# Second layer's values of two and a half token blocks by seven products, with weights' sums made as attention begins

## The chip, the cores and the metric

The kernel runs on one core of one Trainium2 chip. The metric is the device time of one execution in microseconds (us); smaller is better. Before the change the median of three runs is 1869.21 us (1868.77 to 1869.33).

## The reference

Two identical layers, each an attention block followed by a gated linear unit, on 2048 tokens of 448 features in float32; both layers use the same weights. There are 16 heads of 28 features.

```python
qkv = (x @ wqkv).reshape(B, S, 3, H, Dh).transpose(2, 0, 3, 1, 4)
q, k, v = qkv[0], qkv[1], qkv[2]
scores = jnp.einsum("bhqd,bhkd->bhqk", q, k) * (Dh ** -0.5)
o = jnp.einsum("bhqk,bhkd->bhqd", _softmax(scores), v)
attn = o.transpose(0, 2, 1, 3).reshape(B, S, D) @ wo
# glu: (sigmoid(x @ w_gate) * (x @ w_up)) @ w_down
x = x + attn(_layernorm(x)); x = x + glu(_layernorm(x))   # twice
```

## The kernel before

Float32 products are made from float16 pieces: each operand is a high and a low part, and a product is high x high + high x low + low x high. The tokens lie in four blocks of 512 (`Block`, b = 0 to 3), each of four tiles of 128 (j = 0 to 3); the 448 features lie in three chunks of 128 and a tail of 64, whose high and low parts share the 128 rows.

**Stages.** For each layer: `project` makes queries, keys and values of all four blocks; `attend` runs 16 heads; then follow the output projection and the gated unit. Layer 0's attention begins at about 117 us, layer 1's projection runs from about 944 to 1037 us.

**Queries and keys by seven products.** In layer 1 `qk_sums` forms them by a Strassen-like scheme: a 2 x 2 split of features and columns, seven products in place of eight, with sums of weights made beforehand (`split_sums`, `add_up`: 13 operations on DVE and 3 copies on POOL for one set of 28 tiles) and sums of activations made by `Block.half_steps` (r11, t1, t2, t3, r21, t4, r22, r12, last_low, last_rows). The activations' sums lie in the tiles `xwide` (four) and `xshort`. Each product goes to a `chain` bank, which adds up and is copied out by ACT several times on the way, or to a `side` bank, which DVE adds in.

**Squares.** Each finished tile of queries and keys is split (`qkhl`), stored, squared on ACT (`sq`) and reduced by two max operations on DVE; short matmuls on PE (`norms`) then make norms of them, from which comes a bound on the scores. With `defer=True`, `qk_sums` leaves a part of its last operations to be called from outside (`fin(False)`); otherwise it does them itself before it returns. `fin()` reads the norms' peaks.

**Values.** `values_product` makes one tile of 128 tokens: 11 matmuls of 448 columns, `vp<-wv,x`, with the tokens as the stationary operand, so each has a weight load of 128 x 128 tokens. `vals` runs it over tiles and copies the bank out (ACT in general, DVE where a bank is named); it calls what stands in `after` behind a tile. The weights lie in `wv`, the tail's in `wv_tail`, which shares the tile `wsums`. The steps of block three (`h3`) run between those tiles of block one and the query products of block two.

**The end of `project`.** After the four blocks' queries and keys, `vals(2, ...)` makes block two's values; behind its second tile comes `guard_of_norms` (bound, guard row, write to `g_scr`), behind its fourth `worst_of_heads` (a small matmul `bounds`, and DVE's `flag`). Then ACT loads its exponential (`warm`), two tiles of block three follow, and all engines read `flag` and branch (`loose`; the branch isn't taken here). Behind the branch SP loads head 0's guard rows and head 1, and the third tile is made. The fourth is made inside the attention (`last_values`).

**The attention's start.** `attend` issues scores in groups of three tiles on PE (`sc`), exponentials on ACT (`prob`), and the products with the values (`acc`). Some score tiles per head go to DVE instead (`score_aside`: nine operations on `aside`, `expo`, `whole`, `power`); their PSUM bank is shared by the next aside of that head. `last_values` is called around the third group. PE's order is fixed by the order of the code, as is every engine's: each runs its instructions in order.

**Storage.** SBUF tiles come from numbered slots, taken from the front of a list and put back at its end (`Slots`); a tile that takes a slot waits for the last reader of the one before it. In layer 0 `split_v` frees the raw weights.

## Time and profile before

| | before |
|---|---|
| median of 3 runs | 1869.21 us |
| the profiled execution's own time | 1869.45 us |
| its span | 1867.7 us |
| PE busy | 1861.4 us |
| ACT busy | 1404.2 us |
| DVE busy | 1462.4 us |
| granted TensorE clock | 1.00 |

A row of the timeline begins with its start in us from the span's start and its length, then engine, line, operation, output and inputs with their shapes, and xN for N like instructions that follow each other; in brackets is how long the engine was idle before and who released it. A row of the waits' chain has start, length, engine, and the group. A row by source line has shortest, median and longest duration in ns, then first and last start. PE is TensorE's matmul, PEld its weight load, PEq and SPq the sequencers. A window's row gives the engines' busy us and counts, the granted clock, the share of the DMA engines and GB/s. A row of DMA issues ends in the KB of one and the median us from issue to landing.

### The profile page before, as it was taken

The numbers are of one execution on the slowest core, as the hardware profiler recorded it, in microseconds if no ns is written. First come the engines' busy times: TensorE is split into PE (matmuls) and PEld (weight loads), VectorE is DVE, ScalarE is ACT, GpSimd is POOL, SyncE is SP. The second block draws the span as 40 slices with busy tenths as digits, with TensorE's granted clock in tenths as the row PEclk, the third lists the DMA queues.
The fourth block names the chain that finished last, engine by engine and source line by source line (L and its number), as shares of the span: only waits on it lengthen the run. The fifth ranks groups of instructions, "written<-read, shape, count | busy, mean of one in ns | idle before, by whom it ended". The sixth has DMA issues, their size and how long they took to land. (4 is left out here: it accounts for less than half of the span.)

```text
span 1867.7 us, 57157 instructions
## 1 busy us (share of the span) xinstructions
PE 1861.4 (100%) x24479; PEld 1416.1 (76%) x24479; DVE 1462.4 (78%) x2933; ACT 1404.2 (75%) x1865; POOL 306.4 (16%) x582
## 2 busy tenths in 40 slices
PE   9999999999999999999999999999999999999999
PEld 4455566656565899999987568888877668999999
DVE  7748898998997888788877477777777688887764
ACT  6569999999993655555567899999999746555541
POOL 3001123453412111212122000000000031121110
PEclk9999999999999999999999999999999999999999
DMA  7674454454433866757764322122120258677653
GB/s 265 182 214 130 131 160 128 125 156 113 136 129 86 288 211 229 244 204 257 243 187 109 88 52 52 27 53 52 30 50 14 79 165 264 210 249 239 235 201 144
DMA packets 114885, 286.24 MB, mean 153 GB/s; under 512 B 15134, under 2 KB 68878, under 8 KB 114496
## 3 DMA queue, kind: packets, MB, share of 16 engines
q0 software_dynamic: 35088, 174.86, 27.8%
q1 hardware_dynamic: 78384, 106.27, 20.3%
q8 instruction: 194, 3.18, 0.7%
q10 hardware_dynamic: 1152, 1.38, 0.3%
q14 instruction: 67, 0.55, 0.1%
HBM read 218.20 MB, written 54.29 MB: 146 GB/s over the span
## 5 line engine op out<-in xcount | busy, mean ns | idle before, releaser
L1574 ACT ACTIVATE prob_s<-sc 128x1536 f32<-128x1536 f32 (+1 forms) x657 | 888.1, 1484 | 5.9 <-PE sc L1559 3.0
L1609 PE MATMUL acc<-prob_s,val_s 128*32 128x256 f32 (+3 forms) x7708 | 587.2, 384 | 0.0
L1559 PE MATMUL sc<-qp_s 114*32 114x512 f16 x7868 | 571.3, 379 | 0.0
L1559 PEld LDWEIGHTS <-qp_s 114*32 114x32 f16 x8192 | 309.9, 96 | 168.8 <-issue 70.8
L1609 PEld LDWEIGHTS acc<-prob_s,val_s 128*32 128x32 f32 x7708 | 314.1, 110 | 100.3 <-issue 9.2
L1944 PE MATMUL dnp<-dn_s,hparts_s 128*128 128x224 f16 x2184 | 245.8, 259 | 0.0
L664 PEld LDWEIGHTS <-gue_s 128*128 128x128 f16 x2240 | 218.8, 98 | 24.5 <-PE op L1738 0.7
L1944 PEld LDWEIGHTS <-hparts_s 128*128 128x128 f16 x2184 | 210.2, 98 | 5.1
L664 PEld LDWEIGHTS <-gul_s 128*128 128x128 f16 x2016 | 197.0, 98 | 19.9
L664 PE MATMUL chain<-xwide_s,gue_s 128*128 128x256 f16 x1680 | 210.9, 273 | 0.0
L1589 DVE SCALAR_TENSOR_TENSOR power_q<-power_q,expo_q 128x512 f32<-128x512 f32 x243 | 168.2, 692 | 8.3
L664 PE MATMUL side<-xshort_s,gul_s 128*128 128x256 f16 x1344 | 165.0, 273 | 0.0
L2017 ACT COPY one_q<-chain 128x256 f32<-128x256 f32 x224 | 83.1, 372 | 105.4 <-PE chain L664 104.6
L2033 DVE TENSOR_TENSOR one_q<-side,one_q 128x512 f32<-128x512 f32 x112 | 74.3, 689 | 39.1 <-PE side L664 38.8
L1638 DVE STREAM_TRANSPOSE oturned_q<-acc 128x512 f32<-128x512 f32 x32 | 23.0, 717 | 98.4 <-PE acc L1609 98.2
L2044 ACT ACTIVATE one_q<-one_q 128x512 f32<-128x512 f32 x56 | 35.3, 630 | 79.8 <-DVE one_q L2033 79.8
L1609 PE MATMUL acc<-power_q,val_s 128*32 128x256 f32 (+3 forms) x300 | 94.2, 396 | 0.0
L1584 DVE TENSOR_SCALAR expo_q<-aside,base 128x512 f32<-128x512 f32 x81 | 60.6, 748 | 40.5 <-PE aside L1559 40.1
L587 POOL TENSOR_SCALAR rs<-mv 128x1 f32<-128x1 f32 x8 | 1.5, 191 | 505.8 <-DVE mv L585 505.8
L664 PE MATMUL chain<-xshort_s,gul_s 128*128 128x256 f16 x672 | 82.5, 273 | 0.0
L1902 DVE TENSOR_TENSOR hparts_s<-hsums_q,hparts_s 128x256 f16<-128x256 f32 (+1 forms) x152 | 71.3, 519 | 11.1 <-ACT hparts_s L1898 11.1
L664 PE MATMUL side<-xwide_s,gue_s 128*128 128x256 f16 x560 | 79.4, 273 | 0.0
(273 smaller groups left out, 2559.0 us busy)
## 6 DMA issues: line engine op xcount, KB each, us to landing
gue_s<-gu_early POOLq DMA_DIRECT2D x52, 960.0 KB, 5.3
gul_s<-gu_late POOLq DMA_DIRECT2D x52, 768.0 KB, 4.7
dn_s<-dn_parts POOLq DMA_DIRECT2D x42, 784.0 KB, 6.7
qp_s<-qk_scr SPq DMA_DIRECT2D x96, 224.0 KB
xt_scr<-xs_s SPq DMA_DIRECT2D x48, 224.0 KB
xraw_s<-xt_scr SPq DMA_DIRECT2D x12, 768.0 KB
qk_scr<-qkhl_q SPq DMA_DIRECT2D x28, 256.0 KB
qp_s<-qk_scr SPq DMA_DIRECT2D x64, 112.0 KB
```

The costliest lines, as they stand in the source:

```text
L664: nc.tensor.matmul(pm, a, x, start=(first and i == 0), stop=(i == len(terms) - 1), skip_group_check=True)
L1559: nc.tensor.matmul(ps[32 * j:32 * j + 32, :], hd.k[:, keys], hd.q[:, qb * W:(qb + 1) * W], start=True, stop=True, tile_position=(0, 32 * j))
L1574: nc.scalar.activation(prob[:, 0:n, :], ps[:, 0:n, :], AF.Exp, scale=exp_scale)
L1584: nc.vector.tensor_scalar(y, ps, base2[:, 0:1], -116.0, op0=ALU.mult, op1=ALU.max)
L1589: nc.vector.scalar_tensor_tensor(p, p, c[k], y, op0=ALU.add, op1=ALU.mult)
L1609: nc.tensor.matmul(acc[qb * VC:(qb + 1) * VC, s], v[:, kc % TB, h, :], probs[c * NB + qb][:, s], start=(kc == 0 and a == 0), stop=(kc == N ...
L1638: nc.vector.transpose(turned.rearrange("p b c -> p (b c)"), acc)
L1902: nc.vector.tensor_tensor(to[:, :, 1], a, to[:, :, 0], op=ALU.subtract)
L1944: nc.tensor.matmul(pm, a[:, x, t], w[:, p, y], start=(begin and n == 0 and (j == 0 or alone)), stop=(n == 2), skip_group_check=True)
L2017: nc.scalar.copy(to, pm)
L2033: nc.vector.tensor_tensor(one[m], side[m], one[m], op=ALU.add)
L2044: nc.scalar.activation(out, v, AF.Sigmoid, scale=gate_scale)
```

## The change

**Values by sevens.** In layer 1, the values of blocks one and two and of tiles 0 and 2 of block three are made by the seven products of `terms_of_halves`: tiles t and t + 2 together, 128 tokens at a time, 38 matmuls of 224 columns for two tiles in place of 22 of 448. The order of products is 0, 1, 2, 4, 3, 5, 6, with two groups taken in turn in `by_sevens`. ACT copies the chain bank out after products 0, 2, 3 and 5; DVE adds the side bank after 3, 4 and 6.

**Weights' sums.** `split_values(0)` and `(1)` make them from the raw value weights in layer 0's attention, on either side of the last value tile, and POOL writes them to `vs_early` and `vs_late`; `load_products` loads them at the start of layer 1's projection. The raw weights are held until then, with the tail in the first place.

**Orders.** `qk_sums(1)` leaves its squares to run between the value products; `h3` moves later; the guard's zero rows are written earlier; at the end of layer 1's projection the order is tile 1 of block three, block two, the products 0, 1, `worst_of_heads`, product 2 of block three's half, the branch, then products 3 to 6.

```diff
+        def split_values(self, j):
+            t = big.get("vpack", [P, N_SUMS, DV], F16)
+            v = self.raw[2].rearrange("p s (z h n) -> p s z h n", z=2, h=2)[:, :, :, j]
+            split_sums(t, v, up[:, 2:3])
+            for to, a, b in ((vs_early[:, j, 0:7], 1, 8), (vs_early[:, j, 7:EARLY], 14, 22),
+                             (vs_late[:, j, 0:6], 8, 14), (vs_late[:, j, 6:LATE], 22, 28)):
+                nc.gpsimd.dma_start(to, t[:, a:b])
+            big.put(t)
...
+        class Values:
...
+            def product(self, k, pm):
+                c = slice(self.s * P, self.s * P + P)
+                pm = pm.rearrange("p (j n) -> p j n", j=2)
+                terms = terms_of_halves(wq.part, self.blk, k)
+                for i, (a, x) in enumerate(terms):
+                    nc.tensor.matmul(pm, x[:, c], a, start=(k < 2 and i == 0),
+                                     stop=(i == len(terms) - 1), skip_group_check=True)
...
+            def on_chain(self, k, z, t):
+                self.product(k, self.chain)
+                nc.scalar.activation(self.to(z, t), self.of(self.chain), AF.Copy, scale=PS)
+
+            def plus(self, i, z, t):
+                v = self.to(z, t)
+                nc.vector.scalar_tensor_tensor(v, self.of(self.side[i]), PS, v, op0=ALU.mult,
+                                               op1=ALU.add)
...
+        def by_sevens(b, blk, after):
+            groups = [Values(b, blk, s, ((0, 1), (2, 3))[s]) for s in range(2)]
+            for k in (0, 1, 2, 4, 3, 5, 6):
+                for g in groups:
+                    g.do(k)
+                for do in after.get(k, ()):
+                    do()
+            blk.drop()
...
-            fin = qk_sums(1, b1, {0: h2[6:7], 1: h2[7:8], 3: h2[8:9], 4: h2[9:10]})
-            vals(1, b1, {1: both(fin, h3[0]), 2: both(*h3[1:3]), 3: both(*h3[3:5])}, banks=order)
-            fin = qk_sums(2, b2, {0: h3[5:6], 1: h3[6:7], 2: h3[7:8], 3: h3[8:9], 4: h3[9:10]},
+            fin = qk_sums(1, b1, {0: h2[6:7], 1: h2[7:8], 3: h2[8:9], 4: h2[9:10]}, None, True)
+            todo = lambda fin=fin: fin(False)
+            by_sevens(1, b1, {0: [todo], 1: [todo], 2: [todo, h3[0]], 4: h3[1:2], 3: [todo],
+                              5: h3[2:3], 6: [fin]})
+            fin = qk_sums(2, b2, {0: h3[3:5], 1: h3[5:6], 2: h3[6:7], 3: h3[7:8], 4: h3[8:10]},
...
-        vals(2, blks[2], {layer: guard_of_norms, 3: worst_of_heads})
-        nc.scalar.activation(warm, warm, AF.Exp)
-        vals(3, blks[3], {}, range(2))
...
+            vals(3, b3, {}, [1], banks={1: 4})
+            by_sevens(2, b2, {1: [guard_of_norms]})
+            group = Values(3, b3, 0, (6, 7))
+            group.do(0)
+            nc.scalar.activation(warm, warm, AF.Exp)
+            group.do(1)
+            worst_of_heads()
+            group.do(2)
         loose = nc.values_load(flag[0:1, 0:1], min_val=0, max_val=1)
...
-        vals(3, blks[3], {}, [2], 0 if layer == 0 else 7)
+        if layer == 0:
+            vals(3, blks[3], {}, [2], 0)
+        else:
+            for k in (3, 4, 5, 6):
+                group.do(k)
...
         begun = last_values()
+        if layer == 0:
+            wq.split_values(0)
...
             if g == 2:
                 last_values(begun)
+                if layer == 0:
+                    wq.split_values(1)
```

On ACT, behind block one's last query and key products in layer 1, before the change (line, operation, output<-inputs, shape; `val_s` are the copied values):

```order
L957 ACTIVATE sq_q_19484<-qkhl_q_19410 128x512
L957 ACTIVATE sq_q_19488<-qkhl_q_19467 128x512
L941 ACTIVATE qkhl_q_19492<-two_q_19380 128x512
L957 ACTIVATE sq_q_19497<-qkhl_q_19472 128x512
L957 ACTIVATE sq_q_19501<-qkhl_q_19492 128x512
L1136 ACTIVATE val_s_18869<-vp_19505 128x16x28
L477 CAST xwide_s_19546<-xraw_s_19254 128x256 x2
L1136 ACTIVATE val_s_18869<-vp_19518 128x16x28
L479 CAST xwide_s_19546<-t_q_19547 128x512
```

and after it, at the same place:

```order
L1001 ACTIVATE sq_q_19537<-qkhl_q_19463 128x512
L1209 ACTIVATE val_s_18918<-vchain_19541 128x8x28
L1209 ACTIVATE val_s_18918<-vchain_19543 128x8x28
L1001 ACTIVATE sq_q_19557<-qkhl_q_19520 128x512
L985 ACTIVATE qkhl_q_19571<-two_q_19433 128x512
L1209 ACTIVATE val_s_18918<-vchain_19541 128x8x28
L1209 ACTIVATE val_s_18918<-vchain_19543 128x8x28
L1001 ACTIVATE sq_q_19588<-qkhl_q_19525 128x512
L480 CAST xwide_s_19592<-xraw_s_19307 128x256 x2
L482 CAST xwide_s_19592<-t_q_19593 128x512
L1209 ACTIVATE val_s_18918<-vchain_19541 128x8x28
L1209 ACTIVATE val_s_18918<-vchain_19543 128x8x28
```

The copies of the chain banks now stand between the squares, and the third pair of them behind the cast of `t_q`. On DVE at that place, after the change:

```order
L989 SCALAR_TENSOR_TENSOR qkhl_q_19571<-two_q_19433,qkhl_q_19571 128x512
L1005 TENSOR_TENSOR sq_q_19588<-sq_q_19588 128x2x128
L1005 TENSOR_TENSOR sq_q_19588<-sq_q_19588 128x2x64
L472 TENSOR_TENSOR t_q_19593<-xraw_s_19307 128x256 x2
L1213 SCALAR_TENSOR_TENSOR val_s_18918<-vside_19542,val_s_18918 128x8x28
L1213 SCALAR_TENSOR_TENSOR val_s_18918<-vside_19544,val_s_18918 128x8x28
```

There `t_q` stands behind two max operations, and the first additions of the side banks behind it. On PE at the end of layer 1's projection, after the change, between the small matmul `bounds` and the reading of the flag:

```order
L1344 MATMUL bounds_20350<-ident,bnd_20199 1x16
L1198 LDWEIGHTS xwide_s_19592
L1198 MATMUL vchain_20336<-vse_s_18931,xwide_s_19592 128x224
...
L1198 LDWEIGHTS xwide_s_19592
L1198 MATMUL vchain_20336<-vse_s_18931,xwide_s_19592 128x224
L1362 TENSOR_LOAD flag_20200
L1363 COMPARE_AND_BRANCH
```

The lines left out are three more such pairs: five matmuls of 224 stand there now, where 22 of 448 stood. On DVE at the start of layer 0's attention, before the change (`val_s` are the copies of block three's third and fourth tile of values, `aside` the first score tile that DVE takes):

```order
L1138 TENSOR_SCALAR val_s_234<-vp_4856 128x16x28
L1138 TENSOR_SCALAR val_s_234<-vp_4903 128x16x28
L1584 TENSOR_SCALAR expo_q_5002<-aside_4997,base_104 128x512
L1585 TENSOR_SCALAR whole_q_5003<-expo_q_5002 128x512
L1586 TENSOR_TENSOR expo_q_5002<-expo_q_5002,whole_q_5003 128x512
```

and after it (the two tiles `vpack_s` take the same slot one after the other):

```order
L292 TENSOR_TENSOR vpack_s_4913<-vpack_s_4913 64x112
L1182 TENSOR_SCALAR val_s_236<-vp_4906 128x16x28
L269 TENSOR_TENSOR sums_q_4966<-wraw_s_158 128x224
L269 TENSOR_TENSOR sums_q_4966<-sums_q_4966,wraw_s_158 128x224
L269 TENSOR_TENSOR sums_q_4967<-wraw_s_158 128x224
L269 TENSOR_TENSOR sums_q_4967<-wraw_s_158,sums_q_4966 128x224
L275 TENSOR_SCALAR vpack_s_4965<-wraw_s_158,up 128x224
...
L292 TENSOR_TENSOR vpack_s_4965<-vpack_s_4965 64x112
L1689 TENSOR_SCALAR expo_q_5051<-aside_5046,base_106 128x512
```

Before the change `expo_q<-aside,base` followed directly on the copy `val_s<-vp`; now thirteen operations stand between them, and thirteen ahead of that copy.

109 lines of the change are left out of this document (79 added, 30 removed).

## The prediction

> **What bounds the kernel now.** I read the page's busy times first, then the chain that ended last, then windows over the stages that the change touches.
>
> ```profile
> PE 1861.4 (100%) x24479; PEld 1416.1 (76%) x24479; DVE 1462.4 (78%) x2933; ACT 1404.2 (75%) x1865; POOL 306.4 (16%) x582
> PE 44%; DVE 0%; issue 0%
> core 0: us, PE busy (x) PEld busy (x) DVE busy (x) ACT busy (x) POOL busy (x), PEclk, DMA share, GB/s
> 982.50:991.30 8.80, 8.80 (x61) 4.76 (x59) 7.92 (x24) 6.96 (x15) 2.08 (x3) 1.00 0.36 99
> 1021.80:1030.80 9.00, 9.00 (x62) 4.73 (x59) 5.44 (x17) 5.15 (x11) 5.42 (x7) 1.00 0.61 166
> 121.50:149.20 27.70, 27.70 (x524) 16.03 (x520) 16.71 (x31) 27.37 (x22) 2.13 (x4) 1.00 0.80 262
> ```
>
> PE is busy throughout, and the part of the chain that the view resolves is PE's. Time falls by what is taken from PE and rises by any hole made in it. The first window is the second layer's values of block one (counted from zero, as in the code): PE full, but DVE at 7.92 of 8.80 us and ACT at 6.96, so little room for more of their work. The second is the same for block two, with room. The third is the first head of layer 0's attention: ACT 27.37 of 27.70, so PE and ACT are both full; only DVE has 11 us free.
>
> **1. The products.** Gone are 44 matmuls of 448 columns for each of blocks one and two and 22 for half of block three: 110. In their place stand 76, 76 and 38: 190 of 224 columns.
>
> ```profile
> 1036.40 1.14 PE vp L1118 x6
> 1835.21 29.34 PE dnp L1944 x306
> L1944 PEld LDWEIGHTS <-hparts_s 128*128 128x128 f16 x2184 | 210.2, 98 | 5.1
> ```
>
> The first row gives 1.14/6 = 0.190 us for one of 448; the second has the very shape that is added (224 columns, a 128x128 load each): 29.34/306 = 0.0959 us. 110 x 0.190 = 20.9, 190 x 0.0959 = 18.2: **-2.6 us**, -1.0 for each whole block and -0.5 for the half. That is all the change can gain. The third row shows 80 more loads of 98 ns; they cost nothing where they run beside matmuls, as 306 pairs in 29.34 us do (98 + 96 in turn would be 59).
>
> [...]
>
> **2. Block one: squares between products.** The seven products of a token tile share two banks. The chain bank is copied out by ACT after the first, third, fifth and sixth in order, and a product that adds to it waits for the copy; a side bank waits for DVE. I set 0 at 982.46, where these values begin. The two groups alternate, five or six matmuls each: the fifth products end at 4.98, the sixth at 6.13, the seventh at 7.28, without the 14 short norm matmuls (0.44).
>
> ```profile
> 982.46 0.73 PE L1118 MATMUL vp<-wv_s,xwide_s 128*128 128x448 f16 x3
> 982.27 0.60 ACT L941 ACTIVATE qkhl_q<-alone 128x512 f16<-128x512 f32 x1
> 983.28 1.15 ACT L957 ACTIVATE sq_q<-qkhl_q 128x512 bf16<-128x512 f16 x2
> 986.14 0.52 ACT L1136 ACTIVATE val_s<-vp 128x448 f32<-128x448 f32 x1
> 988.48 0.62 ACT L479 CAST xwide_s<-t_q 128x512 f16<-128x512 f32 x1 [0.77 <-DVE t_q L469]
> 984.45 1.01 DVE L961 TENSOR_TENSOR sq_q<-sq_q 128x256 bf16<-128x256 bf16 x4
> 987.71 0.74 DVE L469 TENSOR_TENSOR t_q<-xraw_s 128x256 f32<-128x256 f32 x2
> 992.67 0.63 ACT L981 COPY one_q<-chain 128x256 f32<-128x256 f32 x2
> ```
>
> In the new order a cast of t_q stands on ACT before the two copies after the fifth product. It waits for a DVE pair (0.74), which stands behind two max operations (0.50), which wait for ACT's square of one_q (0.58). Ahead of that square ACT has three activations of 512 (about 0.5 apart), two squares (1.15) and four copies (0.32 to 0.35 each, from the pair of 256 in 0.63): about 4.4 from 982.27, so the square ends near 4.8, the pair at 6.0, the cast at 6.4 or, with the pipelining that the overlapping rows show, 5.9, and the first copy at 6.2 to 6.8. The sixth product would start at about 5.0 and waits 1.2 to 1.8. I take the low end: the rows' starts lie closer than their durations. DVE's addition into the side bank ends near 7.65, so the seventh waits some 0.3 more: **+1.6**. The steps of block three, spread over later tables, take DVE's and ACT's room in the two next products; no row shows them late, and I take 0, with one more DVE pair (0.74) as the worst and the old spacing as the best.
>
> **3. Block two** has the same turns with idle neighbours: copy 0.35, about 0.3 for the last matmul to end and PE to restart, against a cover of about 0.5: **+0.1**, and 0.2 for the norms that now come before tile one's products: **+0.3**. The guard's zero memset and its write start earlier on POOL; nothing on PE waits for them.
>
> **4. The branch.** PE reads the flag, and idles from there unless it has work queued.
>
> ```profile
> 1030.68 0.20 PE L1254 MATMUL bounds<-ident,bnd 16*1 16x16 f32 x2
> 1031.19 0.20 DVE L1256 TENSOR_SCALAR flag<-worst,back 1x1 int32<-1x1 f32 x1
> L1262 PEldq TENSOR_LOAD <-flag x2: 491/510/529, 110.6 to 1031.6; - x2
> L1263 PEldq COMPARE_BRANCH  x2: 367/378/388, 111.2 to 1032.2; - x2
> 1033.85 1.30 PE L1118 MATMUL vp<-wv_s,xshort_s 128*128 128x448 f16 x6
> 1035.29 0.73 PE L1118 MATMUL vp<-wv_s,xshort_s 128*128 128x448 f16 x3
> 1029.81 0.57 POOL L1249 DMA_DIRECT2D g_scr<-guard_s  x1 [1.07 <-DVE guard_s L1247]
> 1037.46 1.48 PE L1559 MATMUL sc<-qp_s 114*32 114x512 f16 x24
> ```
>
> Before, 22 products of 448 (4.2 us) follow the bounds, and the hole after them is 0.30 (1033.85 + 6 x 0.190 = 1034.99, to 1035.29). Now five products of 224 follow: 0.48. The flag comes 0.71 after the bounds' start (1031.39), the compare ends 1.2 later (1032.6), and I add 0.55 until a matmul runs, an estimate: not less than the old hole of 0.30, where only this step was left, and no row shows more than that; less 0.2 for the bounds and 0.48 of products, PE idles 1.78: **+1.5** over the old hole. The four products left after the branch take 2.2, as the old tile does (2.17), and cover the guard rows' load: issued after the flag on SP, it must land before the first scores (1037.46 now). It lands about level; if not, up to 2 more.
>
> **5. The weights' sums in layer 0.** These are 26 operations on DVE, six copies and eight writes on POOL, and two tiles that share one slot.
>
> ```profile
> 116.62 0.62 DVE L1138 TENSOR_SCALAR val_s<-vp 128x448 f32<-128x448 f32 x1 [6.26 <-PE vp L672]
> 121.08 0.62 DVE L1138 TENSOR_SCALAR val_s<-vp 128x448 f32<-128x448 f32 x1 [3.84 <-PE vp L672]
> 124.46 0.75 DVE L1584 TENSOR_SCALAR expo_q<-aside,base 128x512 f32<-128x512 f32 x1 [2.75 <-PE aside L1559]
> 133.41 0.40 PE L1559 MATMUL aside<-qp_s 114*32 114x512 f16 x4
> 255.18 0.42 DVE L266 TENSOR_TENSOR sums_q<-raws_s 128x256 f32<-128x256 f32 x1
> ...
> 260.61 0.22 DVE L289 TENSOR_TENSOR pack_s<-pack_s 64x128 f16<-64x128 f16 x1
> 260.64 0.34 POOL L288 COPY pack_s<-pack_s 64x128 f16<-64x128 f16 x1 [2.73 <-DVE pack_s L275]
> 261.69 0.61 POOL L291 COPY pack_s<-pack_s 64x512 f16<-64x512 f16 x1
> 262.60 0.55 POOL L1442 DMA_DIRECT2D qs_parts<-pack_s  x1 [0.30 <-POOL pack_s L291]
> gu_early<-pack_s POOLq DMA_DIRECT2D x14, 224.0 KB, 2.3
> dn_parts<-pack_s POOLq DMA_DIRECT2D x2, 896.0 KB, 6.0
> 125.00:130.00 5.00, 5.00 (x104) 2.99 (x97) 4.76 (x9) 5.00 (x5) 0.00 (x0) 1.00 1.04 311
> ```
>
> The same thirteen operations on 128 columns take 5.65 us (255.18 to 260.83), so 5.1 on 112. The first set runs from 117.2 to 122.3, then the tile-3 value copy (123.0), then the second set's four sums (124.3). Its first write into the pack tile waits until the four writes of the first set have landed, L. POOL's copies end at about 123.9, and its four issues take until 125.9; with 2.3 to 6.0 us from issue to landing, L is 128.2 to 131.9. Then 3.9 us of splitting follow, and the first step of aside tile one (0.75), which before stood at 124.46 and frees the bank that PE's next aside needs at 133.41. PE loses L + 4.65 - 133.41, that is **L - 128.8**; the in-order PE then starves ACT too, which has no slack. The DMA engines are full in these 5 us (share 1.04), so I take L = 130.5: **+1.75** (0 to 3.1). DVE's 10 us later come out of its 11 free ones.
>
> [...]
>
> ```profile
> L1118 PE MATMUL vp<-wv_s,xwide_s x24: 352/352/362, 958.8 to 1033.3; 128*128 128x448 f16 x24
> ```
>
> The loads of the products' weights (1.5 MB) are issued ahead of block zero's sums, so before 958.8, where block zero's values begin, and are first used at 982.46. At 99 GB/s, the rate of the first window with its DMA share of 0.36, they take 16 us: nothing.
>
> **Sum.** 1869.45 (the profiled execution; its span is 1867.7) - 2.6 + 1.6 + 0.3 + 1.5 + 1.75 = 1872.0. The median before is 0.24 less, so 1871.75 against it; I forecast **1871.8**.
>
> **Rivals.** (a) The sums hide: L under 128.8 (for it the 2.3 row; against it the full DMA engines). Only parts 1 to 4 remain: 1869.2 + 0.8 = 1870.0. (b) The gain stands: ACT's and DVE's orders overlap better than the rows say, block one stalls 0.3 instead of 1.6, and the sums hide: 1869.2 - 2.6 + 0.3 + 0.3 + 1.5 = 1868.7; with the branch at half its price 1868.0. (c) **Clearly slower:** the first set's writes land late, decided from L = 131.7 on. Then PE and ACT stand for 2.9 or more: 1869.2 + 0.8 + 2.9 = 1872.9 and up; with 6.0 us landings and the guard load late by 1, 1874.2. For it speaks the 6.0 row, against it that these writes are a quarter of its size. (d) Each new weight load costs its 98 ns: 80 x 0.098 = 7.8 us, 1879.6; the row of 306 excludes it nearly. [...]
>
> **How the numbers follow.** Measurement tells about 0.2% here, 3.7 us: faster begins under 1865.5, slower over 1872.9. Forecast 0.42, (a) 0.19, (b) 0.17, (c) 0.21, (d) 0.01. Faster by 3.7 is more than all the PE work removed; I leave 0.02 out of (b). So faster 0.02, slower 0.22, the rest 0.76. The range takes (b) in to 1867.6 and (c) to 1874.4; it leaves out some 2 in 10.
>
> **What would show it.** 190 rows of values at 0.096; in block one ACT's two copies after the fifth product at about +6 us and a PE hole of 1.2 before the sixth; a hole of 1.8 at the branch; in layer 0 DVE idle before the second pack write, its end with the pack writes' landing, and a PE hole at the second aside. The forecast is wrong if PE has no hole at 133, if the guard load comes after the last product, or if a later aside lacks its power.

## The result, and the profile after

| | before | after |
|---|---|---|
| median | 1869.35 us (6 runs, 1868.77 to 1869.56) | 1885.05 us (6 runs, 1881.23 to 1889.96) |
| the profiled execution, its span | 1869.45, 1867.7 | 1882.43, 1880.6 |

The ratio is 1.0085, with a 95% interval of 1.0069 to 1.0100: slower by 15.7 us, where 1871.8 was forecast and 1874.4 was the upper end of the range. The runs after also lie 8.7 us apart, those before 0.8 us; the profile is of the second fastest of the six. Three single runs far above all others (2152.88 us of one of the kernels below; 2429.39 and 5079.67 us of before, run beside others) are left out of the figures.

PE is still the bound. This is the page's row of busy times after:

```profile
PE 1861.2 (99%) x24559; PEld 1360.3 (72%) x24559; DVE 1478.0 (79%) x2973; ACT 1405.4 (75%) x1876; POOL 315.9 (17%) x599
```

PE is busy 1861.2 us, against 1861.4 before, while the span grew by 12.9: it stands idle for 19.4 us in place of 6.3. That the 2.6 us saved by the products don't show in its busy time has its reason below (in a window at clock 0.50 PE counts as busy for 4.20 of 4.20 us). The next table divides the span by the starts of the first matmuls of each stage, and gives the change from before to after in us:

| to the first scores of layer 0 | attention 0 | out-projection and gated unit 0 | project 1 | attention 1 | the rest |
|---|---|---|---|---|---|
| +1.58 | **+7.74** | 0.00 | **+2.65** | -0.04 | +0.90 |

**Attention 0.** The timeline of after, DVE's rows first, then POOL's and SP's issues, then PE:

```profile
125.86 0.38 DVE L269 TENSOR_TENSOR sums_q<-wraw_s,sums_q 128x224 f32<-128x224 f32 x1
...
135.82 0.34 DVE L275 TENSOR_SCALAR vpack_s<-wraw_s,up 128x224 f16<-128x224 f32 x1 [9.59 <-DMA vs_late<-vpack_s]
...
139.67 0.75 DVE L1689 TENSOR_SCALAR expo_q<-aside,base 128x512 f32<-128x512 f32 x1
...
125.34 1.14 POOL L767 DMA_DIRECT2D vs_early<-vpack_s  x2
126.47 1.07 POOL L767 DMA_DIRECT2D vs_late<-vpack_s  x2
...
123.52 0.84 SPq L788 DMA_DIRECT2D qk_parts<-wqk_s  x2
124.41 0.99 SPq L789 DMA_DIRECT2D v_parts<-wv_s  x1
...
140.48 0.62 PE L1664 MATMUL aside<-qp_s 114*32 114x512 f16 x4 [5.30 <-DVE expo_q L1689]
```

DVE idles for 9.59 us: the second set's first write into the pack tile stands behind the first set's DMAs, which land at 135.8. That is L of the prediction; in before's time (the stage begins 1.58 later) it is 134.2 where 130.5 was taken. The aside's first step follows 3.85 us later, as foreseen, and PE stands idle for 5.30 us. POOL issues the four writes at 125.3 to 127.5, the last by 126.0 in before's time, where 125.9 was foreseen: all of the lateness is the landing. The view of DMA issues has it, for 116 to 137 us (KB of one, then the median us from issue to landing):

```profile
vs_late<-vpack_s POOLq DMA_DIRECT2D x2, 168.0 KB, 8.7
vs_early<-vpack_s POOLq DMA_DIRECT2D x1, 224.0 KB, 8.8
```

Just ahead of them SP issues the writes of layer 0's weight pieces (`qk_parts`, `v_parts`, 2.75 MB). Before has the same writes at the same place, in a row of its timeline that the prediction doesn't show:

```profile
123.60 0.83 SPq L752 DMA_DIRECT2D qk_parts<-wqk_s  x2
```

The windows of after tell the rest (engines' busy us and counts, granted clock, DMA share, GB/s):

```profile
128.00:133.00 5.00, 5.00 (x96) 2.81 (x85) 0.00 (x0) 5.00 (x5) 0.00 (x0) 1.00 1.02 390
135.00:140.50 5.50, 0.20 (x8) 0.02 (x5) 4.58 (x11) 1.98 (x2) 0.94 (x3) 0.78 0.47 112
140.50:144.70 4.20, 4.20 (x41) 1.94 (x44) 4.03 (x6) 0.93 (x1) 3.66 (x7) 0.50 0.60 193
144.70:149.00 4.30, 4.30 (x88) 2.54 (x84) 4.13 (x8) 3.75 (x4) 1.30 (x2) 0.97 0.93 322
```

While the writes are on their way the DMA engines are full (1.02). Behind the hole PE's clock is 0.50 for 4.2 us: 41 matmuls there, 88 in the 4.3 us after. Half of 4.2 us is 2.1 us lost, and 5.3 + 2.1 = 7.4 of the stage's 7.74. In the same profile the clock is 1.00 behind the hole of 1.65 at the branch; the shifted kernel, below, has half clock behind holes of only 1.0 and 0.9.

**Project 1.** The rows of PE in after that show a hole, and the two at the branch around one:

```profile
997.99 1.31 PE L1198 MATMUL vchain<-vsl_s,xshort_s 128*128 128x224 f16 x12 [1.06 <-ACT val_s L1209]
1018.53 0.38 PE L669 MATMUL side<-xwide_s,wsums_s 128*128 128x256 f16 x2 [1.17 <-DMA xwide_s<-xshort_s]
...
1043.74 0.65 PE L1198 MATMUL vchain<-vse_s,xwide_s 128*128 128x224 f16 x5
1046.05 0.64 PE L1198 MATMUL vchain<-vse_s,xwide_s 128*128 128x224 f16 x5 [1.65 <-PEq L1363]
1047.56 0.73 PE L1198 MATMUL vside<-vsl_s,xshort_s 128*128 128x224 f16 x6 [0.87 <-DVE val_s L1213]
1048.77 0.73 PE L1198 MATMUL vside<-vsl_s,xshort_s 128*128 128x224 f16 x6
1049.44 1.48 PE L1664 MATMUL sc<-qp_s 114*32 114x512 f16 x24
```

The first is block one's sixth product; the second comes from the steps of block three that moved (`h3`): SP issues the tail's low rows (`xwide<-xshort`) later, and the side bank of the next query products waits for them. The third is the branch (L1363). The fourth is new too: product 4 writes the side bank that DVE's addition of product 3 still reads, since 3 and 4 follow each other in the group that stands alone.

**To the first scores.** +0.74 is already there at the first query product (11.88 before). That start differs from profile to profile of all the kernels below by -0.15 to +1.23, so I read nothing in it. The other +0.84 is in layer 0's projection: `split_v` now splits the tail and chunk 0 in its first half and chunks 1 and 2 in its second, and PE waits for chunk 1's low part (the first row).

```profile
31.89 0.35 PE L681 MATMUL vp<-wv_s,xhl_s 128*128 128x448 f16 x1 [0.33 <-DVE wv_s L253]
61.34 0.35 PE L680 MATMUL vp<-wv_s,xhl_s 128*128 128x448 f16 x1 [0.30 <-DVE qkhl_q L928]
```

The second hole comes from DVE's order at 58 to 61 us: the query tile's second part comes 1.7 us later there than before (60.63 and 58.91) while the value products there start only 1.1 later; where that 0.6 comes from stays open. The last column, +0.90, is in this profile a load (`xraw_s<-xt_scr`, at 1715 us); it shows in two other profiles and in none of the rest, and is not settled.

### The profile page after: what moved, and what is told of

Read it like the earlier page. It is cut to its first block, busy times and chain, and to the rows that moved or that the text cites. A ratio compares the mean times of both kernels' runs of the same rounds, so it can differ in the third digit from the quotient of the medians.

```text
span 1880.6 us, 57400 instructions
## 1 busy us (share of the span) xinstructions
PE 1861.2 (99%) x24559; PEld 1360.3 (72%) x24559; DVE 1478.0 (79%) x2973; ACT 1405.4 (75%) x1876; POOL 315.9 (17%) x599
## 5 line engine op out<-in xcount | busy, mean ns | idle before, releaser
L1714 PE MATMUL acc<-prob_s,val_s 128*32 128x256 f32 (+3 forms) x7708 | 573.8, 384 | 0.0
L1664 PE MATMUL sc<-qp_s 114*32 114x512 f16 x7868 | 557.0, 379 | 0.0
L1664 PEld LDWEIGHTS <-qp_s 114*32 114x32 f16 x8192 | 279.1, 96 | 203.1 <-issue 90.2
L1714 PEld LDWEIGHTS acc<-prob_s,val_s 128*32 128x32 f32 x7708 | 279.7, 110 | 134.1 <-issue 11.9
```

The lines of the kernel that those rows point to most:

```text
L1664: nc.tensor.matmul(ps[32 * j:32 * j + 32, :], hd.k[:, keys], hd.q[:, qb * W:(qb + 1) * W], start=True, stop=True, tile_position=(0, 32 * j))
L1714: nc.tensor.matmul(acc[qb * VC:(qb + 1) * VC, s], v[:, kc % TB, h, :], probs[c * NB + qb][:, s], start=(kc == 0 and a == 0), stop=(kc == N ...
```

## The experiments

Each kernel is after with an edit, unless it says before. The changes by stage are those of the profiled execution against the profile of before.

### The writes and the slot

The theory: DVE's wait is for the slot, and what it costs is the hole and the half clock. The first edit gives the second pack tile its own slot (both slots go back after the second set):

```diff
-            big.put(t)
             if j:
-                big.put(self.raw[2])
+                big.put(self.pack, t, self.raw[2])
+            self.pack = t
```

> The changed kernel, with the two pack tiles of layer 0 in two slots. Slot theory: the second set no longer waits for the first set's writes; the PE hole of 5.5 us at the second aside and the 4 us at half clock behind it (2.2 us) go, about 7.7 us; left is the second layer's projection at +2.7 over before and what varies from run to run: 1872 to 1874.5, and the spread of the runs falls from 8 us to about 1. Rival, that the added 10 us of DVE work and the DMA traffic make the asides late whatever the slot: the hole stays at 4 us or more and the time within 3 us of 1885.

Measured: 1878.77 us (1874.23 to 1879.44), ratio 1.0043 [1.0029, 1.0057]. Attention 0 changes by +0.06 in place of +7.74; the aside's step and PE's row, from the timeline of this kernel:

```profile
129.36 0.75 DVE L1689 TENSOR_SCALAR expo_q<-aside,base 128x512 f32<-128x512 f32 x1
134.27 0.40 PE L1664 MATMUL aside<-qp_s 114*32 114x512 f16 x4
```

All sums, copies and writes are still made, so none of those 7.7 us was their work. But the 1872 to 1874.5 us and the small spread that were expected didn't come: the total is some 5 us too high, in project 1 (+6.84). A second thing was at work there, taken up below.

The next kernel is the reverse: slot and sums of after, the second layer's values and order of before (the sums are written and not used). Two more put nothing but idle DVE operations into before, ahead of the same aside, to make a hole of known size:

```diff
-            by_sevens(1, b1, {0: [todo], 1: [todo], 2: [todo, h3[0]], 4: h3[1:2], 3: [todo],
-                              5: h3[2:3], 6: [fin]})
+            vals(1, b1, {1: both(fin, h3[0]), 2: both(*h3[1:3]), 3: both(*h3[3:5])}, banks=order)
...
+                    for _ in range(32):
+                        nc.vector.tensor_scalar(idle, idle, 1.0, None, op0=ALU.mult)
```

> The changed kernel with the second layer's values and orders of before: only the weights' sums in layer 0's attention are added (they are not used). Slot theory: all of the layer-0 loss stays, the projection's 2.7 us go: 1877 to 1887, with the wide spread. Rival, that the loss is in the second layer: 1871 or less.

> The kernel before, with 32 idle DVE operations (about 0.45 us each) ahead of the first aside of layer 0: PE should stand about 2 to 4 us at the second aside. If the clock halves only after a long enough hole, the time rises by the hole alone: 1871.5 to 1873.5. If any hole of microseconds halves it: 2 us more, 1873.5 to 1875.5.

> As s_32 with 40 operations: a hole of 5.5 to 7.5 us. If the half clock of the changed kernel comes from the hole itself: the granted clock is 0.5 for about 4 us behind it and the time rises by the hole and 2.2: 1877 to 1879. If it comes from something else in the changed kernel (its DMA or DVE work): clock 1.0 and 1875 to 1877.

| | median us (range) | ratio | hole | attention 0 | project 1 |
|---|---|---|---|---|---|
| sums only | 1878.47 (1877.31 to 1878.61) | 1.0049 [1.0032, 1.0066] | 5.1 | +7.20 | +0.01 |
| before, 32 operations | 1875.39 (1874.76 to 1876.33) | 1.0031 [1.0016, 1.0046] | 4.1 | +7.10 | +0.01 |
| before, 40 operations | 1879.17 (two runs) | 1.0052 [1.0032, 1.0072] | 7.8 | +9.99 | 0.00 |

The windows of before with 32 operations, in the hole and behind it:

```profile
133.30:137.60 4.30, 0.22 (x6) 0.00 (x0) 4.06 (x9) 2.02 (x2) 0.00 (x0) 0.88 0.58 215
137.60:141.90 4.30, 4.24 (x41) 1.93 (x44) 4.09 (x8) 0.95 (x1) 0.00 (x0) 0.50 0.58 170
```

There is no write of weight sums in this kernel, yet the same 41 matmuls stand at clock 0.50. Each hole costs itself and 2.1 to 3.0 us more, the one of 7.8 no more than the shorter ones. The 32 operations were meant to make a hole of 2 to 4 us; it became 4.1, so these two don't tell whether a shorter one halves the clock. The layer 0 term is settled up to the landing: slot, hole, half clock. The sums-only kernel spreads by only 1.3 us (four runs), where a wide spread was expected, and the two-slot kernel, without the hole, by 5.2: most of after's 8.7 seems to come from layer 1.

Does the landing come late because of SP's writes? Two edits of after keep the single slot. The first moves SP's writes (and the preparation behind them) to a later place in the code; the second has POOL issue them, behind both sets:

```diff
-            if layer == 0 and c == 2:
+            if layer == 0 and c == 8:
                 wq.keep()
...
-                nc.sync.dma_start(qk_parts[i], self.qk[i])
-            nc.sync.dma_start(v_parts, self.v)
+                nc.gpsimd.dma_start(qk_parts[i], self.qk[i])
+            nc.gpsimd.dma_start(v_parts, self.v)
```

> The changed kernel with its one slot, but the 2.75 MB of writes that keep layer 0's weight pieces (SP, at 123.5 to 125.4) and the preparation behind them moved some 8 us later. Theory that the pack writes are late because they share the DMA engines with those writes: they land within 4 us of their issue, by 131.5, and PE's hole at the second aside falls from 5.5 to 1.5 or less. Rival, that they are slow by themselves or behind the head loads: they land at 134 or later and the hole stays over 4.

> The changed kernel with its one slot, but the 2.75 MB of writes that keep layer 0's weight pieces issued by POOL behind both sets' writes, not by SP at 123 us. (In e3_keep_c8 they were not moved: SP still issued them at 122.7.) Theory that the first set's writes are late because they share the DMA engines with these: they land within 4 us of their issue, by 131, and PE's hole at the second aside falls from 5.3 to under 2, without a half clock behind it. Rival, that they are slow for another reason: landing at 133 or later, hole over 4.

The first tells nothing of the writes: 1886.53 us (two runs), ratio 1.0092 [1.0072, 1.0113]. SP reached the writes at the same time, because it waits for nothing on the way; its row:

```profile
122.73 0.83 SPq L788 DMA_DIRECT2D qk_parts<-wqk_s  x2
```

The second: 1884.9 us (two runs), ratio 1.0083 [1.0065, 1.0101]. Its issues and landings, 118 to 137 us, then rows of its timeline on DVE and PE:

```profile
vs_early<-vpack_s POOLq DMA_DIRECT2D x2, 224.0 KB, 3.4
vs_early<-vpack_s POOLq DMA_DIRECT2D x2, 196.0 KB, 2.2
vs_late<-vpack_s POOLq DMA_DIRECT2D x2, 168.0 KB, 4.1
```

```profile
131.00 0.34 DVE L275 TENSOR_SCALAR vpack_s<-wraw_s,up 128x224 f16<-128x224 f32 x1 [4.98 <-DMA vs_late<-vpack_s]
135.66 0.40 PE L1664 MATMUL aside<-qp_s 114*32 114x512 f16 x4 [0.69 <-DVE expo_q L1689]
...
155.14 1.15 DVE L1553 CUSTOM_DVE_ANT_0 junk_s<-raw_s,sums 128x896 bf16<-128x896 f32 x1 [1.98 <-DMA raw_s<-in_B_w_gate_dram]
158.08 1.15 DVE L1553 CUSTOM_DVE_ANT_0 junk_s<-raw_s,sums 128x896 bf16<-128x896 f32 x1 [1.60 <-DMA raw_s<-in_B_w_up_dram]
159.35 0.71 DVE L1743 STREAM_TRANSPOSE oturned_q<-acc 128x512 f32<-128x512 f32 x1
160.11 0.62 PE L1664 MATMUL aside<-qp_s 114*32 114x512 f16 x4 [5.42 <-DVE oturned_q L1743]
```

With nothing of SP's in the way the sums land in 2.2 to 4.1 us, about the low part of the prediction's 2.3 to 6.0, and the hole at the second aside shrinks to 0.69. So SP's writes were the cause of 8.7. The time isn't won: the writes are now in the way of the gate weights' loads, DVE waits for these with a head's transposition queued behind, and PE gets its hole of 5.42 at 160 us, with a clock of 0.52 behind it (attention 0 changes by +8.52). It is the same chain with another transfer: the traffic was moved, and an in-order engine waits for it again. Whether a place can be found that delays neither, with the single slot, was not tried.

### The branch

The two-slot kernel left project 1 at +6.84, against +2.65 in after, with the same code there. The two kernels just above have that code too, and changes of +7.46 and +7.21, with holes of 4.20 at the branch: of four profiles of this code, after's is the only one with a short hole. The timeline and windows of the two-slot kernel at the branch:

```profile
1035.25 0.65 PE L1198 MATMUL vchain<-vse_s,xwide_s 128*128 128x224 f16 x5
1040.17 0.73 PE L1198 MATMUL vchain<-vse_s,xwide_s 128*128 128x224 f16 x5 [4.27 <-PEq L1363]
```

```profile
1035.90:1040.10 4.20, 0.01 (x1) 0.00 (x0) 0.00 (x0) 0.96 (x3) 0.00 (x0) 1.00 0.16 31
1040.10:1045.00 4.90, 3.96 (x23) 2.97 (x23) 0.78 (x2) 0.71 (x2) 0.00 (x0) 0.55 0.91 224
```

The hole that was 1.65 in after's profile is 4.27 here, and the clock halves behind it: 4.27 - 1.65 + 0.45 x 4.9 = 4.8 us, enough for the difference of 4.2 between the two kernels' project 1. Four kernels on top of the two slots shorten the wait step by step: `worst_of_heads` earlier; then product 4 ahead of 3; then the steps of block three later and their row transfer earlier (and other halves in `split_v`); then product 0 of block three and product 4 ahead of the branch, so that more work covers it (this one without the other halves; it loads the value weights' tail first instead).

```diff
-            by_sevens(2, b2, {1: [guard_of_norms]})
+            by_sevens(2, b2, {1: [guard_of_norms], 4: [worst_of_heads]})
...
-            for k in (3, 4, 5, 6):
+            for k in (4, 3, 5, 6):
...
-            by_sevens(1, b1, {0: [todo], 1: [todo], 2: [todo, h3[0]], 4: h3[1:2], 3: [todo],
-                              5: h3[2:3], 6: [fin]})
+            by_sevens(1, b1, {0: [todo], 1: [todo], 2: [todo], 3: [todo, h3[0]],
+                              5: h3[1:2], 6: [fin, h3[2]]})
...
+            by_sevens(2, b2, {1: [guard_of_norms], 4: [worst_of_heads], 5: [lambda: group.do(0)]})
...
+            group.do(4)
```

> The kernel with two slots, with the bounds and the flag made behind the fifth products of block two rather than between the products of block three's half. Theory that PE's branch waits for something that takes 1 to 3.5 us and was covered by the 4.2 us of products behind the flag: PE's sequencer meets the flag while more than 3 us of products are queued, the hole of 1.8 to 4.3 us at the branch falls to 0.3 to 1, the half clock behind it goes, and the time falls from 1878.8 to 1871.5 to 1873.5, with a spread under 1.5. Rival, that the branch itself needs an empty PE: the hole stays over 1.5 and the time over 1874.

> As e5_flag_early, with the fourth and fifth products of block three's half in the order of by_sevens (4 ahead of 3). Theory: product 4 writes to the side bank that DVE's first addition still reads, and in the order 3, 4 it waits for ACT's copy and that addition (0.9 to 1.1 us of hole); in the order 4, 3 it doesn't, and one hole of at most 0.5 is left: 0.5 to 1 us less than e5_flag_early. Rival, that the hole is a late start of PE after the branch: no change.

> As e6_flag_tail, with three more edits that show in stages of their own: block three's first step behind the copies of block one's fifth products (theory: the hole of 1.2 us in block one goes); the small row transfer xwide<-xshort issued two steps earlier (the hole of 1.3 us in block three's sums goes); the raw value weights split as chunks 1 and 2, then 0 and 3, since chunk 0 now holds the tail that lands last (0.85 us of layer 0's projection goes). If all holds: 2.6 us of products less and about 0.5 of holes more than before: 1867 to 1868.5, so 1 to 2.4 us faster than before. If the steps only move their waits elsewhere: 1869.5 to 1871.

> As e7_all, with the first product of block three's half pulled ahead of block two's last products and product 4 put ahead of the branch, so that no matmul waits for a copy in the 2.1 us of products ahead of the branch; the tail of the value weights is loaded first instead of the other split. Theory that PE's sequencer stops at a matmul that waits, and so reads the flag only when that matmul starts: now it reads the flag some 2 us before PE runs dry, and the hole of 1.4 to 1.65 us at the branch falls to 0.3 or less: 1869.7 to 1870.7. Rival, that the branch takes its time only from when PE is empty: the hole stays, 1871 to 1872.5.

| two slots and | median us (range) | ratio | project 1 | PE's compare, us |
|---|---|---|---|---|
| flag early | 1873.02 (1871.96 to 1874.77) | 1.0021 [1.0012, 1.0031] | +2.69 | 1.54 |
| and 4 ahead of 3 | 1872.37 (1871.67 to 1874.77) | 1.0018 [1.0008, 1.0027] | +2.22 | 1.45 |
| and block three's steps, row | 1871.68 (1871.19 to 1873.11) | 1.0013 [1.0003, 1.0023] | +0.77 | 1.26 |
| flag, 4 ahead, steps, row and more cover | 1871.31 (1870.45 to 1872.82) | 1.0011 [1.0002, 1.0020] | +0.37 | 2.23 |

The times of the first two are as expected, but the first's hole is 1.49 where 0.3 to 1 was; the third was expected at 1867 to 1868.5 and the fourth at 1869.7 to 1870.7, with a hole of 0.3 or less. The first's project 1 falls from the two-slot kernel's +6.84 to +2.69 with a compare of 1.54 in place of 3.52, but not by reading the flag earlier: PE reads it at 1035.9 in both. DVE had it at 1032.08 in the second of these kernels, and SP and POOL read it at 1032.1, but PE's sequencer read it only at 1035.5, when the product ahead of it, which waits for ACT's copy, had started (1035.49). Rows of the second kernel, the sequencer by line, then DVE and PE:

```profile
L1361 PEldq TENSOR_LOAD <-flag x2: 315/400/485, 111.3 to 1035.5; - x2
```

```profile
1031.88 0.20 DVE L1346 TENSOR_SCALAR flag<-worst,back 1x1 int32<-1x1 f32 x1
...
1035.49 0.64 PE L1198 MATMUL vchain<-vse_s,xwide_s 128*128 128x224 f16 x5
1037.61 0.74 PE L1198 MATMUL vside<-vsl_s,xshort_s 128*128 128x224 f16 x6 [1.48 <-PEq L1362]
1039.27 0.73 PE L1198 MATMUL vchain<-vsl_s,xshort_s 128*128 128x224 f16 x6 [0.45 <-ACT val_s L1209]
```

Product 4 ahead of 3 takes the hole behind the branch from 0.87 to 0.45. The row transfer's hole goes with its earlier issue (project 1 from +2.22 to +0.77). The other halves remove the hole at 31 us, yet layer 0's projection still costs 0.65 there. Block one's wait is moved rather than removed: with `h3[0]` later, the same wait for ACT's squares and casts appears at the next products. From the kernel with more cover:

```profile
995.91 1.25 PE L670 MATMUL chain<-xwide_s,wsums_s 128*128 128x256 f16 x10 [1.06 <-ACT two_q L1026]
```

In that kernel the flag is read at 1033.7, 1.8 us before the last product ahead of the branch ends (1035.52), and yet there is a hole of 0.95: the compare itself takes 2.23 us. It starts at 1034.1, with products still to run, so the rival that the branch takes its time only from when PE is empty is out, though the time is the one it gave. What makes the compare long? The sequencer's rows by line in several kernels (shortest, median, longest ns; the last start is layer 1's) read, one kernel each, after, two slots, more cover:

```profile
L1363 PEldq COMPARE_BRANCH  x2: 393/744/1096, 112.8 to 1044.8; - x2
```

```profile
L1363 PEldq COMPARE_BRANCH  x2: 393/1954/3516, 112.1 to 1036.5; - x2
```

```profile
L1363 PEldq COMPARE_BRANCH  x2: 384/1308/2231, 112.0 to 1034.1; - x2
```

The same instruction takes 0.38 to 0.39 in layer 0 and 1.10, 3.52 and 2.23 in layer 1. In each of the long ones the profile has one packet of 16 KB on an instruction queue there. The view of DMA queues of after, 1042.5 to 1045.9 us (packets, MB, share of the 16 engines):

```profile
q8 instruction: 1, 0.02, 2.4%
```

The packets start at 1043.19, 1037.66 and 1033.72: 1.6 us ahead of the compare, 1.2 after its start, and 0.4 ahead. The compare ends 2.69, 2.35 and 2.6 us after the packet's start. In the six other kernels here with a compare of 1.26 to 3.65 it ends 2.5 to 2.7 us after one, wherever that starts, from 1.45 ahead of the compare to 1.0 behind its start. Before has no packet of this queue in the 10 us ahead of the compare or beside it, and 0.367.

But a packet starts 1.2 us behind the compare's start in before too (1033.39), when the compare has ended, and in every other kernel with a short one. The packets of the two-slot kernel and the two with one slot start at that usual place, with the compare still running (3.52 to 3.65), and why it has not ended there is not shown: their matmuls ahead of the branch are those of after.

The theory was that this packet, taken for a load of PE's code, holds the branch; the rival, that the new order or the missing cover does. Two kernels tell them apart: before, with only the cover gone (`worst_of_heads` behind tile 1 of block three, the branch at its old place in the code); and the two-slot kernel with 48 matmuls of 16 columns put into block one, some 47 us earlier, to move the branch by 96 rows of code.

```diff
-        vals(2, blks[2], {layer: guard_of_norms, 3: worst_of_heads})
+        vals(2, blks[2], {layer: guard_of_norms} if late else {layer: guard_of_norms, 3: worst_of_heads})
...
-        vals(3, blks[3], {}, range(2))
+        vals(3, blks[3], {1: worst_of_heads} if late else {}, range(2))
...
+                for i in range(48):
+                    nc.tensor.matmul(pm[0:H, 0:H], ind[:, 0, :], ind[:, 1, :], start=(i == 0),
+                                     stop=(i == 47))
```

> The kernel before, with the bounds and the flag behind the second tile of block three in layer 1, so that no product is queued between the flag and the branch. Theory that the branch takes PE 1.5 to 5 us from the flag when nothing is queued: the hole at the branch is 2.4 to 5.5 us in place of 0.3, the time 1871.5 to 1876, and the runs spread by 2 us or more in place of 0.5. Rival, that the fixed 1.75 us of the prediction hold: 1871.5 to 1872, with a spread under 0.7.

> The kernel with two slots, and 48 tiny matmuls (16 x 16; 96 rows of PE's program) ahead of the wait for ACT's copies in block one, where PE stands 1.2 us anyway. In the traces so far PE's compare-and-branch of layer 1 takes 0.37 us where no 16 KB packet of the instruction queue started in the 10 us ahead of it (before, b1_no_cover), and 1.1 to 3.5 us, to 2.3 to 2.7 us after such a packet's start, where one started near it. Theory: the change moved the end of a code block of PE to just ahead of the branch, and the branch waits for its successor's load; 96 rows more move that end 3 us or more away: the compare takes about 0.4, the hole at the branch 1.7 to 1.9 (the flag alone), no half clock behind it, and the time falls from 1878.8 to 1874 to 1876 with a spread under 1.5. Rival, that the branch's length is that of the changed code or of DMA traffic, wherever the block ends: compare over 1, 1877.5 or more.

Before without cover: 1871.73 us (nine runs, 1871.23 to 1872.51), ratio 1.0011 [1.0001, 1.0021]. Shifted: 1873.0 us (1871.36 to 1880.65), ratio 1.0021 [1.0011, 1.0030]. The compare of each:

```profile
L1264 PEldq COMPARE_BRANCH  x2: 367/380/393, 111.5 to 1036.7; - x2
```

```profile
L1370 PEldq COMPARE_BRANCH  x2: 382/385/388, 112.3 to 1035.7; - x2
```

Both are short. With the code moved by 96 rows the packet starts at 1029.28, well ahead of the branch, and the compare falls from 3.5 to 0.38. The order is that of the two-slot kernel, and before without cover is short too, so neither alone makes it long; the place in the code is the likely cause. The shift isn't free of all else: the small matmuls fill block one's wait, and the row transfer's hole falls from 1.08 to 0.22. With a short compare the branch costs about what the prediction had (a hole of 1.51 for its 1.78); before without cover shows:

```profile
1037.22 0.73 PE L1118 MATMUL vp<-wv_s,xshort_s 128*128 128x448 f16 x3 [1.51 <-PEq L1264]
1040.33 1.02 PE L1560 MATMUL sc<-qp_s 114*32 114x512 f16 x13 [0.86 <-DMA qp_s<-qk_scr]
```

That the packets are PE's code is an estimate from their count: on the page of before their queue has 194 packets and 3.18 MB, which is 16 KB each and 65 bytes for each of PE's 48,958 matmuls and weight loads.

The shifted kernel has a median 5.8 us under the two-slot kernel's, below the 1874 to 1876 that was expected. But one of its ten runs is 1880.65, where a spread under 1.5 was expected, and its profile shows half clock at 1038.4 to 1040.8 behind two holes of only 1.0 and 0.9; that stays unexplained. The first of them is no longer the branch's:

```profile
1036.35 0.64 PE L1198 MATMUL vchain<-vse_s,xwide_s 128*128 128x224 f16 x5 [1.01 <-ACT val_s L1209]
```

The copy that it waits for stands on ACT behind the load of the exponential (`ACT_TABLE_LOAD`, 1.28 us from 1034.55). So with the order of after a hole of 1.0 is left in this profile though the compare is short.

Last, two arrangements meant to be the fastest. The first puts tile 1 of block three behind the branch, and the second takes the one with more cover, 40 small matmuls to shift the code, other halves in `split_v`, and the zero fill of the raw weights' tail moved to the attention:

```diff
-            for k in (3, 4, 5, 6):
-                group.do(k)
+            group.do(3)
+            vals(3, b3, {}, [1], banks={1: 4})
+            for k in (5, 6):
+                group.do(k)
...
-            for kts in (slice(0, 2), slice(2, 4)):
+            for kts in (slice(1, 3), slice(0, 4, 3)):
...
-            nc.gpsimd.memset(self.raw[2][64:P, 0, :], 0.0)
+        if layer == 0:
+            nc.gpsimd.memset(wq.raw[2][64:P, 0, :], 0.0)
```

> As e8_cover, with tile 1 of block three behind the branch (22 rows of PE fewer ahead of it), the norms, bound and flag later by as much, block three's steps spread later in block two's sums, and the memset of the tail rows just ahead of layer 0's attention. Theory (the sequencer runs ahead where no matmul waits; the branch waits for a code block only if one ends just ahead of it): hole at the branch under 0.3, none between the last chain products, about 0.5 for the norms: 1869 to 1870.5. If block three's steps now come too late, a wait of 1 to 2 us shows in block three's sums: 1871 to 1872.

> As e8_cover, with the value weights split as chunks 1 and 2, then 0 and 3, the memset of the tail rows just ahead of layer 0's attention, and 40 tiny matmuls (80 rows of PE's program) ahead of the wait of 1.2 us in block two's sums. Theory: the code block's end is moved off the branch, so the compare takes 0.4 and the hole at the branch is under 0.3 (1.1 less than e8_cover); layer 0's projection is 0.55 less; the tiny matmuls cost nothing, as they stand in a wait: 1869.3 to 1870.1, the same as before. Rival, that the branch's length has nothing to do with its place in the code: compare over 1.1 and 1870.5 or more.

The first: 1871.53 us (1871.0 to 1872.47), ratio 1.0011 [1.0002, 1.0020], where 1869 to 1870.5 was expected. A packet starts at 1031.95 and the compare takes 2.28 of its own, so the branch still leaves a hole of 1.20; two more, 1.03 and 0.80, stand between block two's products. The second: 1870.41 us (1869.84 to 1871.4), against 1869.58 of before beside it, ratio 1.0004 [0.9995, 1.0013]: no difference that can be told, and just above the 1869.3 to 1870.1 that was expected. Its packet starts 3.6 us ahead of the compare, where more cover has 0.4, and its compare takes 0.39 in place of 2.23: a second shift, by 80 rows, that bears out the place in the code. The hole at the branch is 0.15, and project 1 changes by -0.43, the only kernel here in which some of the products' gain is left over. Layer 0's projection still costs it 0.86 (holes of 0.24 and 0.30 at 59 and 62 us); with the same code there the first of these two lost 0.16, so this cost isn't settled. Block one's wait remains. No version tried is faster than before.

## Why the prediction was wrong

1. **Products, -2.6: right** (20.9 - 18.2 is 2.7, a slip of 0.1). In block one ten of 224 columns take 1.12 us and twelve 1.31, so one more takes 0.095; the loads of their weights lie beside them (twelve in 1.15 us from 994.56, beside twelve products from 994.66). PE's busy time is as before because the 2.1 us lost at half clock count in it; in the four kernels built on the two slots, whose granted clock is 1.00, it is 1859.0 to 1860.0, 1.4 to 2.4 less.
2. **Block one, +1.6: the mechanism right, the size nearly.** ACT's copies after the fifth product stand behind the cast of `t_q` as foreseen, and the sixth product waits 1.06 by the row's gap, 1.22 counted from start to start as the prediction counts. The seventh doesn't wait. **Block three's moved steps, 0: wrong.** The row transfer they issue on SP came too late, 1.17 us, beyond the worst of 0.74 that was allowed for DVE alone.
3. **Block two, +0.3:** nothing in the trace contradicts it; its holes are too small to tell.
4. **The branch, +1.5.** In this execution the hole was 1.65 (1.83 from start to start) where 1.78 was given, and that is luck: the compare ended 1.58 after the flag and not 1.2, as it took 1.10 in place of 0.38, and PE restarted 0.15 behind it and not 0.55. The step "the compare ends 1.2 later" failed, because it took for fixed what is not: three other profiles of this code have compares of 3.52 to 3.65, holes of 4.20 to 4.27, and then half clock. What sets the compare's length is likely the packet of 16 KB, from whose start to the compare's end 2.35 to 2.7 us pass in the nine long ones; that is not wholly shown. And the four products behind the branch took 3.39 us (1046.05 to 1049.44) and not 2.2, since product 4 waits 0.87 for the side bank. The guard rows came in time for that; in before without cover PE waits 0.86 for them.
5. **The weights' sums, +1.75: the main step that failed.** "With 2.3 to 6.0 us from issue to landing, L is 128.2 to 131.9" took landings from later heads, whose windows in before have a DMA share of 0.30 to 0.60; here, behind SP's 2.75 MB and with a share of 1.02, they took 8.7 and L was 134.2 in before's time. The prediction saw the full engines (its 1.04) but not whose traffic it was. PE's loss L - 128.8 = 5.4 then gives 5.30 measured, so the chain from L on held. Missing altogether was the half clock behind a hole this long, another 2.1. The rival with late writes, "decided from L = 131.7 on", is what happened, but its 1872.9 to 1874.2 went no further than 6.0 us landings. One set is 0.77 MB (168 + 168 + 196 + 224 KB); with half of that window's 390 GB/s it would have taken 4.0 us, an estimate, and the landing took 8.7. In which order the packets of the two queues went is open, as the views don't give it.

Either of the last two steps is enough to leave the range: the two-slot kernel, without the wait for the slot, has 1878.77 us, and sums only, without the new order, 1878.47.

From the prediction's 1872.0 to the profiled 1882.43: layer 0's attention 7.74 - 1.75 = 6.0, project 1 2.65 - 0.8 = 1.85 (from start to start the row transfer's hole is 1.33 and product 4's 1.03, and block one takes 0.38 less than given), layer 0's projection 0.84, the start 0.74, the load in the last stage 0.90; together 10.3 of 10.4. The median lies 2.6 above the profiled run; that it is the branch's varying wait is likely, as the three profiles with the long hole have 4.2 to 4.8 more in project 1, but not shown for these runs. The slowest, 1889.96, lies 7.5 above the profiled run, more than that explains.

Why is even the best arrangement no faster? The gain of 2.6 had to pay for holes, and most of those in project 1 come from one fact: the matmuls taken away were the cover of something else, the branch, DVE's and ACT's turns, and a transfer. In its own profile project 1 keeps 0.43 of the gain, and layer 0's projection takes 0.86.

## What to carry to other kernels

When an in-order engine waits for a slot, take the landing time from the traffic that will be there at that moment (who else issues within the same microseconds, and how many MB), not from the same transfer elsewhere; and where the wait becomes a hole on PE's path, ask for the clock behind it: behind holes of 4.1 to 7.8 us in layer 0's attention it was halved here, which added 1.6 to 3.0 us to the price. The second slot took 7.7 us away here and left attention 0 at +0.06. Matmuls removed from in front of a branch, a copy or a row transfer were often its cover: count what will be uncovered before counting what is saved.

## What the runs showed of the hardware

- In layer 0's attention a hole of 4.1, 5.1, 5.3, 5.6 (the writes at a later place) or 7.8 us on PE was followed by half clock, and cost 1.6 to 3.0 us more than itself; behind one of 1.65 at the branch the clock was 1.00. The shifted kernel's half clock behind two of 1.0 and 0.9 stays open.
- PE's compare and branch took 0.37 to 0.39 us, or 1.1 to 3.65, and each of the nine long ones ended 2.35 to 2.7 us after the start of a 16 KB packet on an instruction queue. With 80 or 96 rows more ahead of it the compare was short in two kernels (0.39 and 0.38). That the packet is the cause rests on this timing and on the two shifts, which moved some waits too; why the same code has 1.10 in one profile and 3.52 to 3.65 in three is open.
- Writes of 168 to 224 KB landed in 2.2 to 4.1 us where POOL issued SP's writes behind them, and in after, with those 2.75 MB on another queue ahead, in 8.7 to 8.8.
- PE's sequencer did not read the flag ahead of a matmul that still waited for another engine: ready at 1032.08, and read by SP and POOL at 1032.1, it was read by PE at 1035.5, when the product that waited for ACT's copy had started (1035.49). In the kernel with more cover, where no product ahead of the branch waited, it read the flag at 1033.7, 1.8 us before the last of them ended (1035.52).
